# A planned attention and mixture of experts on one core: a new order for the attention, other prices for TensorE's passages, and 32 unread products of ones among the first steps

## The chip, the core and the metric

The kernel runs on one core of a Trainium2 chip. The core has five engines with a queue each: PE (TensorE, the matrix unit), DVE (VectorE), ACT (ScalarE), POOL (GpSimd) and SP (SyncE, which issues most DMAs here). An engine takes its instructions strictly in the order in which the program holds them and waits on semaphores for what the others do. The metric is the device time of one execution in microseconds (us).

## The reference

The first half is attention for 4 batches of 8 heads, 768 positions and head size 64, with a window of 128 positions and 4 positions at the start (sinks) that all see. The second half is a mixture of 8 experts over the 3072 resulting rows of 512 numbers; each row goes to its two best experts.

```python
scores = scale * np.matmul(q, k.transpose(0, 1, 3, 2))
is_sink = pos[None, :] < int(n_sink)
in_window = (rel >= 0) & (rel < int(window))
scores = np.where(is_sink | in_window, scores, -1000000000.0)
a = np.exp(scores - np.max(scores, axis=-1, keepdims=True))
a = a / (np.sum(a, axis=-1, keepdims=True) + 1e-09)
attn = np.matmul(a, v)
...
noisy_logits = x @ w_gate + np.log1p(np.exp(x @ w_noise)) * noise
top2 = np.argpartition(-noisy_logits, 2, axis=1)[:, :2]
...
h = np.maximum(x[mask] @ w1[e], 0.0)
out[mask] += top2_w[mask, k, None] * (h @ w2[e])
```

## The kernel before

**Two plans.** `phase_one` holds the attention, the routing of the first three batches, and the first loads and splits of expert 0. `phase_two` holds the routing of the last batch and the experts. Each phase lists its operations in a `Plan`: engine, duration, priority, function, what it reads and writes. `Plan.run` then plays the list through with those durations, takes on each engine the ready operation with the lowest priority number, and emits the instructions in the order of their planned starts. So the durations and the priorities (the table `PR`) set the order in which the instructions stand on every engine; on the chip that order is fixed, whatever the durations turn out to be.

**The tiles.** A group `g` is a pair of heads of one batch (16 groups); a step `n` is 256 positions of one group (48 steps, three in each group). On PE a step is:

- `turn` (T): q and k are transposed, `turn_c` on ACT copies them to `kq`, `ksink` on POOL adds the sinks' keys;
- `qk` (S): the scores, by matmuls that use 64 rows of the array, two heads at a time (kind 1 in the plan);
- `ptr` (P): the exponentials are transposed, and copied by `ptr_c` on ACT to `CT`; `ptr_m` masks them into `CM`;
- `pctr`: the sinks' part is transposed into tile X, and copied by `sink_c` on ACT to `ps`;
- `pv`: the product with v and with dv (the difference of neighbouring blocks of v, made by POOL or DVE from `vn`), by matmuls that use 64 columns of the array (kind 2), into the same tile X;
- `sinks` (kind 3): the product of `ps` with the sinks' v (`vr`), into X too; `pv_c` on ACT copies X out to `xtn`, `rows` transposes it back, `rows_c` on DVE scales it.

`vr` comes from a tile `st` that 16 small DMAs fill for each batch (`sink_values`), and two operations over all of it (`sink_hi` on ACT, `sink_lo` on DVE).

**The tile X.** `pctr`, `pv`, `sinks` and `rows` of one step write parts of one PSUM tile. The plan holds `pv` and `sink_c` for independent of each other. The program does not: the framework orders reads and writes of a tile as they are emitted. Where `pv` is emitted ahead of `sink_c`, ACT's copy waits for `pv` to end, and `sinks` waits for the copy.

**Passages.** PE's instructions have four forms: 128 rows by 128 columns (transposes, `sinks`), 64 rows (`qk`), 64 columns (`pv`), 32 columns (the gate's projection in `logits`). The plan adds a time when the kind changes, and `stay` (in `PR`) holds the engine on its kind.

**The start.** SP loads k and q of group 0 and 1, then v of group 0 and 1 (`vn`), then the 16 DMAs of `st`. One product of ones (`warm`) is issued ahead of all.

**The end of phase one.** `gather` fetches 4 tiles of rows for expert 0 after the routing of batch 2 (`place`), `rows_turn` transposes them (L947), and the first matmul of an expert is that of L1070.

Of the kernel before, what the change touches and what calls it, by code (L numbers as in the profile page):

```python
# [17 lines left out]
OP = mybir.AluOpType  # L18
AX = mybir.AxisListType
BIG = 1.0e30  # L20
PR = dict(dv_pool=2, cm_pool=10, gap=3, pc_pool=0, warm=1, cur=-28.393, cur1=3.934, cur1_0=-210.795, cur1_9=-0.214,
          cur_0=-6.435, cur_9=42.546, dv=-181.673, dv_0=-58.475, dv_9=-165.981, exps=924.339, exps_0=-284.526,
          exps_9=-135.434, ga=442.815, gt=5.527, ksink=329.474, ksink_9=351.649, lg=5.452, load_qk=4.916, load_v=-10.311,
          mins=-1.124, mins_0=-130.078, mins_9=-231.976, nosink=115.551, nosink_0=201.297, nosink_9=23.605,
          pcopy=-1100.148, pcopy_0=54.064, pcopy_9=13.8, plow=6.687, plow_0=155.036, plow_9=-170.043, prev=-313.725,
          prev_0=560.262, prev_9=8.445, ptr=-158.634, ptr_0=-7.014, ptr_9=481.977, ptr_c=113.881, ptr_c_0=180.788,
          ptr_c_9=110.108, ptr_m=-225.012, ptr_m_0=-135.409, ptr_m_9=-137.504, pv=-1.694, pv_0=1.459, pv_9=2.578,
          pv_c=-36.493, pv_c_0=-19.005, pv_c_9=0.119, qk=-419.785, qk_0=3.807, qk_9=316.006, rows=-857.853,
          rows_0=-458.314, rows_9=34.438, rows_c=-1553.261, rows_c_0=-208.37, rows_c_9=-15.709, rt=-558.501, sink_c=2.596,
          sink_c_0=-90.91, sink_c_9=-279.362, sinks=-714.907, sinks_0=-12.828, sinks_9=261.99, sub=318.235, sub_0=521.605,  # L30
          sub_9=182.999, sums=78.667, sums_0=135.936, sums_9=-1.546, sums_i=-160.405, sums_i_0=280.185, sums_i_9=-301.562,
          t0=11.199, t2=-37.957, tgroup=71.501, tgroup_0=-63.73, tgroup_9=-56.402, tgroup_c=-1595.788, tgroup_c_0=7.035,
          tgroup_c_9=-3.093, w1=579.923, ksink_0=-652.007, stay=3844.16, pctr_0=71.802, sinkv=185.095, sc_dve=2,
          pctr=-325.901, pctr_9=-655.681)
CAP = 832

CAPS = (832, 832, 832, 800, 800, 768, 768, 768)
COLD = 6.0
FIRST = 4
ZEROS = 16  # L40

# [5 lines left out]
class Plan:  # L47
# [16 lines left out]
    def get(self, tag, i, shape=None, dt=F32, pool="sb", pad=None):  # L64
        kx = (tag, i)
        if kx not in self.live:
            more = {"padded_shape": pad} if pad else {}
            self.live[kx] = self.pools[pool].tile(shape, dt, name=tag, bufs=self.rings[tag], **more)
        return self.live[kx]

    def op(self, eng, dur, prio, fn, r=(), w=(), u=(), lat=None, kind=0):


        i = len(self.ops)
        deps = set()
        for kx in list(r) + list(w) + list(u):
            if kx not in self.touch:
                self.touch[kx] = []
                self.wrote[kx] = []
            if kx[0] in self.rings:  # L80
                deps.update(self.touch.get((kx[0], kx[1] - self.rings[kx[0]]), ()))
        for kx in list(r) + list(w):
            deps.update(self.wrote[kx])
        for kx in w:
            deps.update(self.touch[kx])
        for kx in list(r) + list(w) + list(u):
            self.touch[kx].append(i)
        for kx in w:
            self.wrote[kx].append(i)
        self.ops.append((eng, dur, prio, fn, sorted(deps), lat, kind))  # L90
# [10 lines left out]
    def run(self, dry=False):  # L101
        n = len(self.ops)
        left = [len(o[4]) for o in self.ops]
        succ = [[] for _ in range(n)]
        for i, o in enumerate(self.ops):
            for d in o[4]:
                succ[d].append(i)
        at, start, free, pend = [0.0] * n, [0.0] * n, {}, {}
        kind = 0
        for i, o in enumerate(self.ops):  # L110
            free.setdefault(o[0], 0.0)
            pend.setdefault(o[0], ([], []))
            if not left[i]:
                heapq.heappush(pend[o[0]][0], (0.0, i))

        def arrive(e, t):
            wait, ready = pend[e]
            while wait and wait[0][0] <= t:
                _, i = heapq.heappop(wait)
                heapq.heappush(ready, (at[i] if e == "DMA" else self.ops[i][2], i))  # L120

        for _ in range(n):
            best = None
            for e, (wait, ready) in pend.items():
                arrive(e, free[e])
                if ready or wait:
                    t = free[e] if ready else wait[0][0]
                    if best is None or t < best[0]:
                        best = (t, e)
            t, e = best  # L130
            arrive(e, t)
            ready = pend[e][1]
            if e == "PE":
                x = min(ready, key=lambda x: (x[0] + (PR["stay"] if self.ops[x[1]][6] != kind else 0), x[1]))
                ready.remove(x)
                heapq.heapify(ready)
                i = x[1]
            else:
                _, i = heapq.heappop(ready)
            if e == "DVE" and self.ops[i][6]:  # L140
                t = max(t, free["Pool"])
            start[i] = t
            d = self.ops[i][1]
            if e == "PE":
                d = (d + (.25 if self.ops[i][6] == 1 != kind else .1 if self.ops[i][6] != kind else 0)) * (2 if t < self.cold else 1)
                kind = self.ops[i][6]
            elif e == "DVE" and self.ops[i][6]:
                free["Pool"] = t + d
            free[e] = end = t + d
            for s in succ[i]:  # L150
                lat = self.ops[i][5]
                if lat is None:
                    lat = (0 if e == "PE" else .06) if e == self.ops[s][0] else self.LAT.get((e, self.ops[s][0]), .2)
                at[s] = max(at[s], end + lat)
                left[s] -= 1
                if not left[s]:
                    heapq.heappush(pend[self.ops[s][0]][0], (at[s], s))
        self.start, self.free = start, free
        if not dry:
            for i in sorted(range(n), key=lambda i: (start[i], i)):  # L160
                if self.ops[i][3]:
                    self.ops[i][3]()
        return max(free.values())
# [20 lines left out]

def constants(nc, pool, sh):
    c = {}
    c["nz"] = pool.tile([128, sh.T, sh.E], F32, name="nz")
    jp = c["nz"].rearrange("p t e -> p (t e)")[:, :128].bitcast(I32)
    nc.gpsimd.iota(jp, pattern=[[1, 128]], base=0, channel_multiplier=-1)
    c["idf"] = pool.tile([128, 128], F32, name="idf")  # L190
    nc.vector.tensor_scalar(c["idf"], jp, 0.0, None, op0=OP.is_equal)
    c["jp"] = jp
    return c
# [6 lines left out]
def attention(tc, plan, consts, cst, sh, q, k, v, xbuf):  # L200
    nc = tc.nc
# [37 lines left out]
    def warm():  # L239

        one = cst["one"]
        nc.tensor.matmul(get("P", 0, [128, 4, 128], F32, "ps"), one, one[:, None, :].to_broadcast([128, 4, 128]),
                         start=True, stop=True)

    def sink_zero(b):
# [209 lines left out]
    for gi in range(NJ):  # L455
        for nm in nms:
            load(nm, 0, gi, -20 + gi)
    for i in range(PR.get("warm", 16)):
        op("tick", .43 if i else 1.5, i, None, r=[("t", 0)], w=[("t", 0)], lat=0)
        op("PE", .43, 1000, warm, r=[("t", 0)], w=[("P", 0)])  # L460
    for g in range(NP):
        p0 = g * NJ
        e = p0 - NJ
# [24 lines left out]
        for jj in range(NJ):  # L488
# [12 lines left out]
            if not jj:  # L501
# [13 lines left out]
               r=[("P", n + NJ) if me == "DVE" else ("CT", n)], w=[("CM", n)])  # L515
            XA[n] = xa = plan.next("X")
            op("PE", .11, n + .6 + P(g, "pctr"), lambda n=n: pctr(n), r=[("pc", n)], w=[("X", xa)])
            op("PE", .95 if jj else .7, n + .6 + P(g, "pv"), lambda n=n: pv(n),
               r=[("vn", g), ("CT", n), ("dv", g), ("CM", n), ("X", xa)], w=[("X2", xa)], kind=2)
            op("ACT", .17, n + .6 + P(g, "sink_c"), lambda n=n: sink_c(n), r=[("X", xa)], w=[("ps", n)])  # L520
            op("PE", .26, n + .6 + P(g, "sinks"), lambda n=n: sinks(n), r=[("ps", n), ("vr", g // HP)], w=[("X2", xa)], u=[("X", xa)],
               kind=3)
            op("ACT", .27, n + .6 + P(g, "pv_c"), lambda n=n: pv_c(n), r=[("X2", xa)], w=[("xt", n)], u=[("xtn", g), ("X", xa)])
            op("PE", .22, n + .7 + P(g, "rows"), lambda n=n: rows(n), r=[("xt", n), ("ps", n)], w=[("X", xa)], u=[("xtn", g)])
# [6 lines left out]
def routing_setup(nc, pool, tmp, cst, sh, w_gate, w_noise, noise):  # L531
# [19 lines left out]
    iota("dum", [128, 1], [[0, 1]], -128, 1)  # L551
    c["tri"] = tmp.tile([128, 128], BF, name="tri")
    nc.vector.tensor_scalar(c["tri"], c["jp"], 0.0, None, op0=OP.is_gt)
    c["one"] = tmp.tile([128, 128], BF, name="one")
    nc.vector.memset(c["one"], 1.0)


    c["m"] = tmp.tile([128, T + sh.FA, E], BF, name="m")
# [43 lines left out]
def logits(nc, plan, cst, sh, b, jj, z):  # L602
# [29 lines left out]
        nc.vector.tensor_reduce(get("lg", b, [128, NT, 2 * E])[:, 2 * jj:2 * jj + 2, :],  # L632
                                get(*mk).rearrange("p t h e -> p t e h"), op=OP.add, axis=AX.X)

    op("PE", .57, z, proj, r=[("xt", n) for n in ns] + [("gw", x) for x in range(4)], w=[("X", xa)], u=[("xtn", g) for g in pairs])
    op("ACT", .27, z, copy, r=[("X", xa)], w=[tk])
    op("PE", .22, z, turn, r=[tk], w=[("X", xa)])
    op("DVE", .34, z, scale, r=[("X", xa)] + [("rin", n) for n in ns], w=[mk], u=[("ri", b)])
# [750 lines left out]
```

## Time and profile before

| | |
|---|---|
| median of three runs | 801.34 us (800.09 to 804.37) |
| span of the profiled execution | 802.8 us |
| that execution's own time beside its span | not given apart; the span stands for it, 1.5 us above the median |
| PE busy in that span | 772.3 us (96%), 4753 matmuls |
| DVE, ACT, POOL busy | 434.3, 342.6, 441.5 us |
| first matmul of an expert (L1070) | 220.09 us after the start |

The views used: rows of the timeline give start, length, engine, line, operation and tiles, and in brackets how long the engine stood idle ahead of it and what ended that. Rows that follow each other are merged (x8 is eight). A matmul's shown length is its way through the array, so several overlap; what PE pays for one is the distance from start to start. An instruction on fp32 data is recorded in as many parts as the hardware makes of it, so that `pv`'s eight matmuls are sixteen records and start in pairs. Windows give for a stretch its length and the busy time of each engine in turn (PE, PE's weight loads, DVE, ACT, POOL), then PE's granted clock and the DMA's share and rate.

### The profile page before, as it was taken

To read this page: it belongs to the slowest core of one execution; us is meant where nothing else is said; L and a number is where in the kernel's file an instruction comes from. 1 tells how busy PE (TensorE), PEld (TensorE's weight loads), DVE (VectorE), ACT (ScalarE), POOL (GpSimd) and SP (SyncE) were. 2 spreads that over 40 slices of the span, in tenths; PEclk is the share of its full clock that TensorE was granted. 3 is DMA by queue.
4 is the path that set the end of the run, shared out by engine and by line. 5 is a ranking of instruction groups with operands and counts; after the bars stand their busy time and mean duration, and the time that the engine had idled before them with its cause. 6 is when DMAs were issued, how large, how long until landed. Compare 5 with 4: busy or idle time off the path is not lost.

```text
span 802.8 us, 13806 instructions
## 1 busy us (share of the span) xinstructions
PE 772.3 (96%) x4753; PEld 656.1 (82%) x4753; DVE 434.3 (54%) x1115; ACT 342.6 (43%) x695; POOL 441.5 (55%) x669
## 2 busy tenths in 40 slices
PE   7999999899798999999999999999999999999996
PEld 4776777677577888988988898899889999999994
DVE  5888897798565345354435434542553363364320
ACT  5877778686420334244233413332442343334121
POOL 5757657778604447473745456374636647366222
PEclk9999999999999999999999999999999999999998
DMA  6769767845526196264526535561744365174133
GB/s 121 169 150 200 162 155 207 181 120 129 152 90 175 22 257 152 45 140 128 102 38 158 141 56 94 144 119 37 147 123 94 73 172 121 26 175 97 32 40 40
DMA packets 151193, 96.03 MB, mean 120 GB/s; under 512 B 100528, under 2 KB 129200, under 8 KB 151120
## 3 DMA queue, kind: packets, MB, share of 16 engines
q1 hardware_dynamic: 137744, 67.93, 32.6%
q0 software_dynamic: 13376, 27.19, 19.4%
q8 instruction: 38, 0.62, 0.3%
q14 instruction: 35, 0.29, 0.1%
HBM read 66.89 MB, written 28.20 MB: 118 GB/s over the span
## 4 chain that ended last, share of the span: by engine, by line
PE 64%; issue 4%; DMA 2%; POOL 2%; DVE 1%; SPq 0%; ACT 0%; POOLq 0%; DVEq 0%; ACTq 0%
PE H L1070 11%; PE H L1072 10%; PE H L1071 10%; PE Y L1099 10%; PE Y L1101 10%; PE Y L1100 10%; POOL out L1123 1%; PE Y L1104 1%; PE Y L1105 1%; DMA xg<-x_rows,idg 1%; DMA out<-y,idx 1%; DMA st<-in_moe_w 1%; SPq L1268 0%; PE T L947 0%; PE X L616 0%
## 5 line engine op out<-in xcount | busy, mean ns | idle before, releaser
L903 POOL DMA_INDIRECT xg<-x_rows,rt_idq x174 | 175.8, 1010 | 62.1 <-issue 51.7
L1070 PE MATMUL H<-skn,w 128*128 128x384 f32 (+4 forms) x512 | 178.3, 348 | 0.0
L1072 PE MATMUL H<-skn,w 128*128 128x384 f32 (+4 forms) x512 | 176.8, 345 | 0.0
L1071 PE MATMUL H<-sqn,w 128*128 128x384 f32 (+4 forms) x512 | 176.3, 344 | 0.0
L1088 DVE SCALAR_TENSOR_TENSOR h<-H,h 128x384 fp32r<-128x384 f32 (+4 forms) x168 | 75.5, 469 | 184.7 <-ACT h L1081 184.5
L1081 ACT ACTIVATE h<-H 128x384 fp32r<-128x384 f32 (+4 forms) x128 | 64.6, 505 | 249.4 <-PE H L1072 249.3
L1132 POOL COPY spacer<-h 1x1 f32<-1x1 f32 x88 | 26.6, 303 | 167.3 <-ACT h L1081 167.1
L1123 POOL DMA_INDIRECT out<-y,idx x53 | 89.2, 1683 | 50.4 <-ACT y L1108 34.6
L1070 PEld LDWEIGHTS H<-skn,w 128*128 128x128 f32 x512 | 96.6, 189 | 7.7 <-issue 0.8
L1071 PEld LDWEIGHTS H<-sqn,w 128*128 128x128 f32 x512 | 96.6, 189 | 6.9
L1072 PEld LDWEIGHTS H<-skn,w 128*128 128x128 f32 x512 | 96.4, 188 | 3.0
L1101 PE MATMUL Y<-w2b,h 128*128 128x512 f32 x192 | 75.2, 392 | 1.1 <-DVE h L1088 1.1
L1099 PE MATMUL Y<-w2b,h 128*128 128x512 f32 x192 | 75.5, 393 | 0.6 <-ACT h L1081 0.6
L1099 PE MATMUL Y<-w2a,h 128*128 128x512 f32 x192 | 75.5, 393 | 0.0
L1100 PE MATMUL Y<-w2b,h 128*128 128x512 f32 x192 | 75.2, 392 | 0.0
L1100 PE MATMUL Y<-w2a,h 128*128 128x512 f32 x192 | 75.1, 391 | 0.0
L1101 PE MATMUL Y<-w2a,h 128*128 128x512 f32 x192 | 74.9, 390 | 0.0
L197 POOL TENSOR_TENSOR cbuf<-cbuf,mn 128x528 f32<-128x528 f32 x48 | 52.6, 1098 | 18.5 <-DVE mn L330 10.7
L310 PE MATMUL S<-kq 64*128 64x264 f32 (+1 forms) x384 | 56.4, 410 | 1.0 <-DVE ri L348 0.5
L961 ACT ACTIVATE skn<-xtn 128x512 fp32r<-128x512 f32 (+2 forms) x46 | 27.9, 606 | 63.3 <-DVE xtn L952 63.2
L197 DVE TENSOR_TENSOR w<-st,w 128x1024 fp32r<-128x1024 f32 x28 | 34.3, 1224 | 17.8 <-ACT w L1008 17.8
L1101 PEld LDWEIGHTS Y<-w2b,h 128*128 128x128 f32 x192 | 36.1, 188 | 9.4 <-DVE h L1088 1.6
(209 smaller groups left out, 1359.6 us busy)
## 6 DMA issues: line engine op xcount, KB each, us to landing
st<-in_moe_w SPq DMA_DIRECT2D x36, 512.0 KB
st<-in_moe_w SPq DMA_DIRECT2D x112, 128.0 KB
out<-zt SPq DMA_DIRECT2D x31, 256.0 KB
vn<-in_v SPq DMA_DIRECT2D x16, 384.0 KB
x_rows<-xr SPq DMA_DIRECT2D x48, 128.0 KB
kn<-in_k SPq DMA_DIRECT2D x30, 192.0 KB
qn<-in_q SPq DMA_DIRECT2D x30, 192.0 KB
xg<-x_rows,rt_idq POOLq DMA_INDIRECT x174, 2.9
```

The source lines that it names most:

```text
L197: eng.tensor_tensor(out, a, b, op=OP.subtract)
L310: nc.tensor.matmul(p[:, :2 if j else 1], kq(g)[r, j // 2, 2 + j % 2, NS:], x[:, :2 if j else 1], start=True, stop=True)
L903: nc.gpsimd.indirect_dma_start(out=x[:, i, :], out_offset=None, in_=xbuf.rearrange("r (q d) -> (r q) d", d=sh.SW), in_offset=bass.Indirect ...
L1070: nc.tensor.matmul(p, w[:, 0, i], xh, start=(i == 0), stop=False)
L1071: nc.tensor.matmul(p, w[:, 0, i], xl, start=False, stop=False)
L1072: nc.tensor.matmul(p, w[:, 1, i], xh, start=False, stop=(i == DC - 1))
L1081: nc.scalar.activation(get("h", FC * q + f, [128, 2 * 128 * FIRST], F32R)[:, :width], get("H", FC * q + f), AF.Relu)
L1088: nc.vector.scalar_tensor_tensor(h[:, o:o + s1 - s0], p[:, s0:s1], 0.0, h[:, s0:s1].bitcast(F32), op0=OP.max, op1=OP.subtract)
L1099: nc.tensor.matmul(p, hh, w[:, 0], start=(f == 0), stop=False)
L1100: nc.tensor.matmul(p, hh, w[:, 1], start=False, stop=False)
L1101: nc.tensor.matmul(p, hl, w[:, 0], start=False, stop=(f == FC - 1))
L1123: d = nc.gpsimd.indirect_dma_start(out=out, out_offset=bass.IndirectOffsetOnAxis(ap=c["idx"][:size(e, t), e, t:t + 1], axis=0), in_=get("y ...
```

## The change

`PR` gets other numbers throughout; for steps 0, 1 of every eight `pcopy` is on POOL and not on ACT (`pc_pool=2`: 12 of 48). The plan's price of a passage becomes .2 us into `qk` and .15 us otherwise, kind 0 and 3 count as one, and the gate's projection counts as kind 2. `ones` is written first of all on DVE, and 32 products of ones, which nobody reads, are put into PE's list with the worst priority; each may be planned .215 us after the one ahead of it, and so they fill places in which the plan sees PE idle. They write a tile of the ring X that is used by no step.

```diff
-PR = dict(dv_pool=2, cm_pool=10, gap=3, pc_pool=0, warm=1, cur=-28.393, cur1=3.934, cur1_0=-210.795, cur1_9=-0.214,
+PR = dict(dv_pool=2, cm_pool=10, gap=3, pc_pool=2, cur=-316.098, cur1=74.576, cur1_0=389.469, cur1_9=0.0, cur_0=0.0,
...
-COLD = 6.0
+COLD = 5.0
+WARM = 32
...
-                x = min(ready, key=lambda x: (x[0] + (PR["stay"] if self.ops[x[1]][6] != kind else 0), x[1]))
+                x = min(ready, key=lambda x: (x[0] + (PR["stay"] if self.ops[x[1]][6] % 3 != kind % 3 else 0), x[1]))
...
-                d = (d + (.25 if self.ops[i][6] == 1 != kind else .1 if self.ops[i][6] != kind else 0)) * (2 if t < self.cold else 1)
+                d = (d + (0 if self.ops[i][6] % 3 == kind % 3 else .2 if self.ops[i][6] == 1 else .15)) * (2 if t < self.cold else 1)
...
+    c["one"] = pool.tile([128, 128], BF, name="one")
+    nc.vector.memset(c["one"], 1.0)
...
-        nc.tensor.matmul(get("P", 0, [128, 4, 128], F32, "ps"), one, one[:, None, :].to_broadcast([128, 4, 128]),
+        nc.tensor.matmul(get("X", first, [128, 4, 128], F32, "ps"), one, one[:, None, :].to_broadcast([128, 4, 128]),
...
-    for i in range(PR.get("warm", 16)):
-        op("tick", .43 if i else 1.5, i, None, r=[("t", 0)], w=[("t", 0)], lat=0)
-        op("PE", .43, 1000, warm, r=[("t", 0)], w=[("P", 0)])
+    first = plan.next("X")
+    for i in range(WARM):
+        op("tick", .215 if i else 1.2, i, None, r=[("t", i - 1)], w=[("t", i)], lat=0)
+        op("PE", .215, 1e6, warm, r=[("t", i)], u=[("X", first)])
...
-            op("PE", .95 if jj else .7, n + .6 + P(g, "pv"), lambda n=n: pv(n),
+            op("PE", .87 if jj else .65, n + .6 + P(g, "pv"), lambda n=n: pv(n),
...
-    op("PE", .57, z, proj, r=[("xt", n) for n in ns] + [("gw", x) for x in range(4)], w=[("X", xa)], u=[("xtn", g) for g in pairs])
+    op("PE", .45, z, proj, r=[("xt", n) for n in ns] + [("gw", x) for x in range(4)], w=[("X", xa)], u=[("xtn", g) for g in pairs],
+       kind=0 if last else 2)
```

The lines of the changed kernel are two further down from `attention` on (L310 becomes L312). From the last projection of the gate in phase one on, PE's order is the same row for row in both kernels.

**The start, on SP.** The loads of v (`vn`) and of `st` trade places. Before:

```order
L267 DMA kn<-in_k 128x6x64 x2
L267 DMA qn<-in_q 128x6x64 x2
L271 DMA vn<-in_v 128x12x64 x2
L250 DMA st<-in_v 4x4x64 x16
L267 DMA kn<-in_k 128x6x64 x2
```

And after:

```order
L269 DMA kn<-in_k 128x6x64 x2
L269 DMA qn<-in_q 128x6x64 x2
L252 DMA st<-in_v 4x4x64 x16
L273 DMA vn<-in_v 128x12x64
L269 DMA kn<-in_k 128x6x64 x2
```

The sixteen small loads now stand ahead of v of group 0, and v of group 1 stands behind k and q of group 2.

**The first steps, on PE** (P is `ptr`, X<-pcbuf is `pctr`, X<-CT and X<-CM are `pv`, X<-ps is `sinks`). Before:

```order
L368 MATMUL P<-idf,cbuf 128x128 x4
L394 MATMUL X<-CT,vn 64x128 x4
L397 MATMUL X<-CM,dv 64x128 x2
L310 MATMUL S<-kq 128x264 x4
L385 MATMUL X<-idf,pcbuf 128x128
L394 MATMUL X<-CT,vn 64x128 x4
L397 MATMUL X<-CM,dv 64x128 x4
L406 MATMUL X<-ps,vr 128x128 x4
```

And after, from the last of the 32 products of ones on (five of them stand between the third P and this `pctr`):

```order
L244 MATMUL X<-one 128x512
L387 MATMUL X<-idf,pcbuf 128x128
L396 MATMUL X<-CT,vn 64x128 x4
L399 MATMUL X<-CM,dv 64x128 x2
L396 MATMUL X<-CT,vn 64x128 x4
L399 MATMUL X<-CM,dv 64x128 x4
L408 MATMUL X<-ps,vr 128x128 x4
```

The two steps' `pv` stand together, and the scores of step 4 no longer stand ahead of them.

**The last steps, on PE** (T<-xg is `rows_turn`, X<-xtn is `rows`). Before:

```order
L385 MATMUL X<-idf,pcbuf 128x128
L394 MATMUL X<-CT,vn 64x128 x4
L397 MATMUL X<-CM,dv 64x128 x4
L406 MATMUL X<-ps,vr 128x128 x2
L368 MATMUL P<-idf,cbuf 128x128 x4
L419 MATMUL X<-idf,xtn 128x128 x2
L385 MATMUL X<-idf,pcbuf 128x128
L394 MATMUL X<-CT,vn 64x128 x4
L397 MATMUL X<-CM,dv 64x128 x2
L406 MATMUL X<-ps,vr 128x128 x2
L419 MATMUL X<-idf,xtn 128x128 x2
```

And after:

```order
L387 MATMUL X<-idf,pcbuf 128x128
L396 MATMUL X<-CT,vn 64x128 x4
L399 MATMUL X<-CM,dv 64x128 x4
L387 MATMUL X<-idf,pcbuf 128x128
L408 MATMUL X<-ps,vr 128x128 x2
L396 MATMUL X<-CT,vn 64x128 x4
L399 MATMUL X<-CM,dv 64x128 x2
L408 MATMUL X<-ps,vr 128x128 x2
L421 MATMUL X<-idf,xtn 128x128 x4
L370 MATMUL P<-idf,cbuf 128x128 x4
```

Where each step ran through by itself, two steps now lie in each other: another step's `pctr` stands between a `pv` and its `sinks`, and `rows` come two steps at a time.

More of the change, by code (lines that the diff above doesn't have):

```diff
@@ L20 @@
 BIG = 1.0e30
-PR = dict(dv_pool=2, cm_pool=10, gap=3, pc_pool=0, warm=1, cur=-28.393, cur1=3.934, cur1_0=-210.795, cur1_9=-0.214,
[L22 to L34, printed above, removed]
@@ new lines @@
+PR = dict(dv_pool=2, cm_pool=10, gap=3, pc_pool=2, cur=-316.098, cur1=74.576, cur1_0=389.469, cur1_9=0.0, cur_0=0.0,
+          cur_9=-338.706, dv=3.697, dv_0=-3440.041, dv_9=-5.252, exps=1433.695, exps_0=14.943, exps_9=-47.365,
+          ga=261.653, gt=590.016, ksink=102.577, ksink_9=-11.086, lg=0.317, load_qk=0.0, load_v=-0.697, mins=36.093,
+          mins_0=683.429, mins_9=58.706, nosink=6.145, nosink_0=366.642, nosink_9=-4.22, pcopy=-25.182,
+          pcopy_0=877.155, pcopy_9=-7.293, plow=8.138, plow_0=-19.886, plow_9=-223.574, prev=0.0, prev_0=-19.364,
+          prev_9=0.0, ptr=0.655, ptr_0=-69.919, ptr_9=-0.248, ptr_c=-19.131, ptr_c_0=9.758, ptr_c_9=0.0, ptr_m=-794.5,
+          ptr_m_0=-408.279, ptr_m_9=186.738, pv=606.544, pv_0=-415.362, pv_9=170.355, pv_c=-3.043, pv_c_0=0.0,
+          pv_c_9=5.912, qk=-228.31, qk_0=-195.444, qk_9=299.15, rows=0.0, rows_0=437.256, rows_9=408.894,
+          rows_c=-2103.315, rows_c_0=517.963, rows_c_9=0.0, rt=-680.773, sink_c=-36.416, sink_c_0=35.85,
+          sink_c_9=12.309, sinks=-332.739, sinks_0=-432.619, sinks_9=393.682, sub=65.273, sub_0=-820.977,
+          sub_9=74.172, sums=120.291, sums_0=-696.415, sums_9=977.753, sums_i=0.0, sums_i_0=584.662, sums_i_9=-20.343,
+          t0=-29.656, t2=12.759, tgroup=1036.947, tgroup_0=2.026, tgroup_9=0.0, tgroup_c=323.737, tgroup_c_0=11.405,
+          tgroup_c_9=561.666, w1=1204.601, ksink_0=-1177.388, stay=3039.256, pctr_0=0.0, pctr=-574.631, pctr_9=-0.362)
@@ L517, in attention @@
             op("PE", .11, n + .6 + P(g, "pctr"), lambda n=n: pctr(n), r=[("pc", n)], w=[("X", xa)])
-            op("PE", .95 if jj else .7, n + .6 + P(g, "pv"), lambda n=n: pv(n),
+            op("PE", .87 if jj else .65, n + .6 + P(g, "pv"), lambda n=n: pv(n),
                r=[("vn", g), ("CT", n), ("dv", g), ("CM", n), ("X", xa)], w=[("X2", xa)], kind=2)
             op("ACT", .17, n + .6 + P(g, "sink_c"), lambda n=n: sink_c(n), r=[("X", xa)], w=[("ps", n)])
-            op("PE", .26, n + .6 + P(g, "sinks"), lambda n=n: sinks(n), r=[("ps", n), ("vr", g // HP)], w=[("X2", xa)], u=[("X", xa)],
+            op("PE", .22, n + .6 + P(g, "sinks"), lambda n=n: sinks(n), r=[("ps", n), ("vr", g // HP)], w=[("X2", xa)], u=[("X", xa)],
                kind=3)
@@ L553, in routing_setup @@
     nc.vector.tensor_scalar(c["tri"], c["jp"], 0.0, None, op0=OP.is_gt)
-    c["one"] = tmp.tile([128, 128], BF, name="one")
-    nc.vector.memset(c["one"], 1.0)
     c["m"] = tmp.tile([128, T + sh.FA, E], BF, name="m")
```

## The prediction

> **What bounds the kernel now.** I read the page's busy times and chain first, then windows by stage, then PE's rows where a stage loses time.
>
> ```profile
> span 802.8 us, 13806 instructions
> PE 772.3 (96%) x4753; PEld 656.1 (82%) x4753; DVE 434.3 (54%) x1115; ACT 342.6 (43%) x695; POOL 441.5 (55%) x669
> PE 64%; issue 4%; DMA 2%; POOL 2%; DVE 1%; SPq 0%; ACT 0%; POOLq 0%; DVEq 0%; ACTq 0%
> ```
> ```profile
> 0.00:22.70 22.70, 17.26 (x91) 10.27 (x91) 14.14 (x38) 12.32 (x26) 13.58 (x37) 1.00 0.66 131
> 22.70:198.00 175.30, 168.90 (x1665) 127.34 (x1666) 151.20 (x414) 133.53 (x353) 122.59 (x237) 1.00 0.70 163
> 198.00:220.00 22.00, 15.53 (x150) 11.83 (x148) 13.42 (x34) 9.68 (x23) 13.77 (x18) 0.92 0.54 153
> 220.00:802.80 582.80, 570.63 (x2855) 506.67 (x2851) 255.58 (x631) 187.09 (x294) 291.52 (x380) 0.99 0.47 105
> ```
>
> PE carries everything. The experts (last row) keep the order they have, so what the attention saves moves them forward whole, and what it loses moves them back; their one long wait, for rows gathered after the last routing, hangs on their own start. The attention has three stages: a head with 5.4 us of idle PE, a middle with 6.4 us in 175, and a tail with 6.5 us in 22. In the middle DVE is busy for 151.2 of 175.3 us (86%): there is little room above PE.
>
> **Passages.** The distance from start to start says what PE pays.
>
> ```profile
> 24.79 1.16 PE L310 MATMUL S<-kq 64*128 64x264 f32 x8
> 25.88 0.66 PE L419 MATMUL X<-idf,xtn 128*128 128x128 f32 x4
> 26.37 0.60 PE L368 MATMUL P<-idf,cbuf 128*128 128x128 f32 x4
> 26.81 0.38 PE L283 MATMUL T<-idf,kn 128*128 128x128 f32 x2
> 27.02 0.38 PE L283 MATMUL T<-idf,qn 128*128 128x128 f32 x2
> 27.24 0.27 PE L385 MATMUL X<-idf,pcbuf 128*128 128x128 f32 x1
> 27.45 0.66 PE L394 MATMUL X<-CT,vn 128*64 128x128 f32 x8
> 27.93 0.61 PE L397 MATMUL X<-CM,dv 128*64 128x128 f32 x8
> 28.47 0.33 PE L385 MATMUL X<-idf,pcbuf 128*128 128x128 f32 x1
> 28.64 0.38 PE L283 MATMUL T<-idf,kn 128*128 128x128 f32 x2
> ```
>
> Four transpositions P take .44 us (26.37 to 26.81), .11 each, and T follows for nothing. Into `pv` there is .10 more (27.24 to 27.45 for one of .11) and about .04 within its first eight (.48 for four pairs of .11): .15. Back, .10 (27.93 to 28.47) and .06 (28.47 to 28.64): .16. Scores: four pairs of 264 columns should take .90 by the same rate and take 1.09, which is some .10 at each end, and with the .10 ahead of the entry a passage into them is .2. In PE's rows up to the first L1070 I count 190 passages before, 50 of them into scores, and 176 after, 54 into scores. That is 50 x .2 + 140 x .15 = 31.0 us against 54 x .2 + 122 x .15 = 29.1: **1.9 us off PE**. Passages between 64 and 32 columns, six after and one before, may cost nothing: up to .8 more.
>
> **Copies behind `pv`.** Where `sink_c` is emitted after its step's `pv`, ACT waits for `pv` and `sinks` for ACT:
>
> ```profile
> 120.28 0.61 PE L397 MATMUL X<-CM,dv 128*64 128x128 f32 x8
> 120.94 0.28 ACT L401 ACTIVATE ps<-X 128x128 fp32r<-128x128 f32 x1 [0.65 <-PE X L397]
> 121.27 0.44 PE L406 MATMUL X<-ps,vr 128*128 128x128 f32 x2 [0.38 <-ACT ps L401]
> ```
> ```profile
> ACT ps L401 <- PE X L397: 17.7, 20, 2.5
> ```
>
> `pv`'s four pairs need .44 and the way out .10; `sinks` starts .99 after them, so .45 are lost, and .06 in its first record: .5. In the order of the built programs `sink_c` stands behind its `pv` in 22 of 48 steps before, and in 8 of these `sinks` follows `pv` with nothing between: five in the middle, three in the tail. After, it is 8 steps, and two with nothing between, one in each stage. So the middle gets 4 x .5 = 2.0 back. The second row says that ACT stood 17.7 us behind `pv` in all; all that is queued behind the copy (exponentials, CT, the copies of S) came late too, and with 8 such steps for 22 most of that goes. Of the 4 us of idle PE in the middle that these five do not explain I take 1.4 us as gained. **Middle: 3.4 us**, between 0 (other waits take their place, DVE first) and 6.4 (all idle time).
>
> **The tail.**
>
> ```profile
> 203.89 0.28 ACT L401 ACTIVATE ps<-X 128x128 fp32r<-128x128 f32 x1 [2.47 <-PE X L397]
> 206.15 0.69 DVE L378 TENSOR_TENSOR CM<-P,ge 128x512 f32<-128x512 f32 x1 [3.46 <-ACT CT L371]
> 211.75 0.28 ACT L401 ACTIVATE ps<-X 128x128 fp32r<-128x128 f32 x1 [2.31 <-PE X L397]
> 215.29 0.63 PE L947 MATMUL T<-idf,xg 128*128 128x128 f32 x4 [0.67 <-PE X L385]
> 217.33 0.66 PE L947 MATMUL T<-idf,xg 128*128 128x128 f32 x4
> 219.53 0.64 PE L616 MATMUL X<-xtn,wbd 128*32 128x256 f32 x8 [1.26 <-DVE sqn L197]
> ```
> ```profile
> 210.50:213.90 3.40, 3.03 (x23) 2.63 (x20) 2.58 (x8) 1.52 (x5) 0.78 (x2) 0.51 0.81 211
> ```
>
> Here the late copies do most harm: ACT stands 2.5 and 2.3 us, DVE behind it 3.5, PE is idle for 6.5 and then runs 3.4 us at half its clock (0.51), which costs 1.7: 8.2 in all. After, two steps lie in each other. What stays or is new: the wait ahead of the last projection, 1.3; the third and fourth L947, which stand .2 us of PE work apart where the tile's way over ACT and DVE took 2.04 from start to start (215.29 to 217.33), so some 1.4; two pairs of P with only a `pctr` between, whose copy on ACT takes .6, some 1.5 for both; one late copy, .5. That makes 4.7, **a gain of 3.5 us**. It is 0 if a new chain through the gathers decides (POOL's four follow the same routing product), and 6.9 if only the last wait stays.
>
> **The head.** Two things change.
>
> ```profile
> 7.28 2.69 PE L310 MATMUL S<-kq 64*128 64x132 f32 x12
> 9.89 0.69 PE L283 MATMUL T<-idf,kn 128*128 128x128 f32 x2
> 10.37 0.64 PE L283 MATMUL T<-idf,qn 128*128 128x128 f32 x2
> 10.94 3.51 PE L310 MATMUL S<-kq 64*128 64x264 f32 x12
> 14.38 1.11 PE L368 MATMUL P<-idf,cbuf 128*128 128x128 f32 x4
> 17.62 0.66 PE L368 MATMUL P<-idf,cbuf 128*128 128x128 f32 x4
> 23.97 0.89 PE L406 MATMUL X<-ps,vr 128*128 128x128 f32 x4
> ```
>
> Two T's take .48 here (9.89 to 10.37) and .21 later (26.81 to 27.02), and four P's show 1.11 at 14.38 and .66 at 17.62: up to some 16 us PE runs at half its clock, though the windows' clock column says 1.00. The products of ones keep PE at work from about 1.2 us (ones is now DVE's first work; SP starts at .93 in the row below). They are 128x512, .21 us at the full clock and .43 at half. When the clock comes free then, no row says. It came free after 3.4 us in the tail and in the head some 8.7 us after the scores at 7.28 began, from which on no long wait stands in the rows; so between 4.6 and 10.
>
> By PE's rows, up to the end of the `sinks` of steps 0 and 1 there are 18.1 us at the full clock, 6.9 of them ones. Up to the time t at which the clock comes free, (t - 1.2) / 2 of them is done, and the rest follows at the full clock, so they end at t + 18.1 - (t - 1.2) / 2 = 18.7 + t/2: 21.0 to 23.7. Before, they ended at 24.8 (the row of 23.97), but with one step's scores (1.2 us) done besides; the mark is 24.8 - 1.2 = 23.6. So PE alone would gain up to 2.6.
>
> The other thing is `st`.
>
> ```profile
> 0.93 0.98 SPq L267 DMA_DIRECT2D kn<-in_k  x2
> 9.35 2.40 SPq L271 DMA_DIRECT2D vn<-in_v  x2
> 11.86 7.29 SPq L250 DMA_DIRECT2D st<-in_v  x16
> 21.30 1.05 ACT L254 ACTIVATE vr<-st 128x1024 fp32r<-128x1024 f32 x1
> ```
>
> Its 16 DMAs now start at 9.35 and end between 14.8 (at .34 each, most of them) and 16.6; they land 2.1 later at most (19.15 to 21.30). ACT's queue has `vr` ahead of the exponentials of step 2, which stood behind it before: 16.9 to 18.7, then 1.05 + .6 (a copy of T) + .64, and P of step 2 comes at 19.2 to 21.0. Behind it stand five products of ones (1.1), `pctr`, two `pv`, `sinks`: 4 us, an end at 23.2 to 25.0. v of group 0 goes out behind `st` as well, lands by some 19, and dv needs 1.55 on POOL: no later than that. So the wait for `st` takes what the clock would give: **the head loses .5**, between a gain of 2.6 and, if the clock stays at half all through (37.4), a loss of 13.8.
>
> **Edits with no price of their own.** 12 copies go from ACT to POOL, which is at 70% in the middle. The later priority of expert 0's weights moves splits on ACT and POOL that end ahead of the first expert in both orders. Were POOL's not done, L1070 would wait for them.
>
> **The sum.** 1.9 + 3.4 + 3.5 - .5 = 8.3 us off the profiled execution: 802.8 - 8.3 = 794.5. That execution lies 1.5 above the median of the runs (801.3), so 793.0.
>
> **The rivals.**
>
> - *Only the passages count.* The waits in middle and tail are those of a pipeline whose DVE is 86% busy; taken from ACT they come back as waits for DVE (in the list of PE's waits DVE hardly stands now, which speaks against it). Then 1.9 - .5 = 1.4: 799.9. Chance .14.
> - *Products of ones at half clock ahead of real work* (the other side). Each stands in PE's queue and costs .43 there. With the clock held until t the sinks end at 18.7 + t/2 against 23.6, and the other gains, 8.8, are eaten at t = 27.4. Held all through, 13.8 - 8.8 = 5.0 lost: 806.3. Against it: in the tail 3.4 us sufficed. Chance .05.
> - [...] Chance .12.
> - *Middle and tail lose nearly no time any more*: 5.5 and 6 gained: 788.1. Chance .14.
>
> [...]
>
> **How the numbers follow.** The forecast, with sizes of its terms between half and one and a half, has .50 and a range of 789 to 797; other mixtures of small losses make the last .05, at 802 to 808. A measurement of this kernel tells about .5% (4 us) from no change. Below 797.3 are the forecast, the third rival for the most part, the fourth: .76. Within 4 us are the first and edges of the others: .17. Above 805.3: .07. The range that leaves out 2 in 10 goes from 786 to 801.
>
> **What would show it.** Right: L1070 first at about 212; T's of .21 from about 7 us on; ACT's waits for `pv` ahead of L403 near 6 us; tail windows at a full clock; DVE at about 89% in the middle. Wrong: a first `pv` later than 22 us with ones right ahead of it, new waits of PE for DVE in the middle of several us, or L949's first row held by the gathers.

## The result, and the profile after

The changed kernel takes 797.07 us (median of 16 runs, 794.56 to 801.82), the kernel before 804.46 (16 runs, 800.09 to 808.76): ratio 0.9918, with a 95% interval of 0.9900 to 0.9936. By the ratio that is 6.6 us off (the two medians lie 7.4 apart), where 8.3 were forecast. The time of 797 lies in the range given (786 to 801), though 4 above the 793 named: the three runs of before that were shown have a median 3.1 below that of all 16.

The profiled executions differ by more, 802.8 against 795.4. The page of the changed kernel:

```profile
span 795.4 us, 13881 instructions
PE 772.5 (97%) x4784; PEld 654.8 (82%) x4784; DVE 436.0 (55%) x1115; ACT 341.3 (43%) x683; POOL 439.0 (55%) x681
PE 80%; issue 5%; DVE 4%; POOL 3%; DMA 3%; ACT 3%; SPq 1%; POOLq 0%; DVEq 0%; ACTq 0%
```

PE is as busy as before (772.5 for 772.3) though 6.9 us of products of ones have come in. Windows by stage, cut at four events that both have: the start of the last of the first four `sinks` (steps 0 and 1), the routing product of batch 2 (the matmul `rt_tc,rt_op`), the first expert's matmul, the end. First before, then after (columns as in the prediction: length, then PE, weight loads, DVE, ACT and POOL; near the end PE's granted clock):

```profile
0.00:24.60 24.60, 19.15 (x111) 11.73 (x111) 15.94 (x41) 12.96 (x28) 15.48 (x39) 1.00 0.71 138
24.60:201.76 177.16, 169.27 (x1670) 127.75 (x1671) 152.12 (x415) 134.31 (x355) 123.52 (x238) 1.00 0.69 162
201.76:220.09 18.33, 13.35 (x126) 9.96 (x123) 10.70 (x30) 8.26 (x19) 11.03 (x15) 0.91 0.55 157
220.09:802.80 582.71, 570.54 (x2855) 506.67 (x2851) 255.58 (x631) 187.09 (x294) 291.43 (x380) 0.99 0.47 105
```
```profile
0.00:23.90 23.90, 20.82 (x133) 11.70 (x134) 14.03 (x38) 11.89 (x23) 13.19 (x40) 1.00 0.65 135
23.90:195.62 171.72, 167.82 (x1679) 126.99 (x1679) 154.88 (x417) 133.85 (x347) 125.05 (x250) 1.00 0.72 169
195.62:214.07 18.45, 13.89 (x126) 9.72 (x123) 11.71 (x31) 8.46 (x20) 11.39 (x15) 0.88 0.58 172
214.07:795.40 581.33, 569.95 (x2855) 506.39 (x2851) 255.37 (x630) 187.09 (x294) 289.39 (x378) 1.00 0.45 104
```

The head ends .7 earlier, but without the scores (1.2 us) that before had done by then: .5 lost. The middle is 5.4 shorter, with those scores in it: 6.6 gained. From the routing product to the first expert's matmul nothing moved: 18.33 against 18.45. The experts are 1.4 shorter. The sum is .5 - 6.6 + .1 - 1.4 = -7.4. In the middle PE's idle time falls from 7.9 to 3.9 us (length less busy time); the other 2.6 are less busy time, once the scores' 1.2 are counted on both sides.

The middle: ACT's list of waits up to 220 us, whose first row before was 17.7 us for `pv` ahead of the copy of the sinks' part:

```profile
ACT xtn L416 <- PE X L408: 10.3, 16, 1.4
ACT ps L403 <- PE X L399: 8.6, 7, 1.9
```

It has fallen to half (8.6; near 6 was expected), and `sinks` waits for that copy .8 us in all (two times) for 3.0 (eight times) before.

The head: PE's rows, and POOL's for `dv`:

```profile
1.25 3.17 PE L244 MATMUL X<-one 128*128 128x512 bf16 x7 [1.25 <-DVE one L188]
4.21 0.63 PE L285 MATMUL T<-idf,kn 128*128 128x128 f32 x2
5.10 1.24 PE L244 MATMUL X<-one 128*128 128x512 bf16 x5
...
19.73 1.24 PE L244 MATMUL X<-one 128*128 128x512 bf16 x5
21.03 0.33 PE L387 MATMUL X<-idf,pcbuf 128*128 128x128 f32 x1
21.29 0.66 PE L396 MATMUL X<-CT,vn 128*64 128x128 f32 x8
22.28 0.44 PE L399 MATMUL X<-CM,dv 128*64 128x128 f32 x4 [0.34 <-POOL dv L199]
```
```profile
20.69 1.54 POOL L199 TENSOR_TENSOR dv<-vn 128x640 f32<-128x640 f32 x1 [3.91 <-DMA vn<-in_v]
```

Seven products take 3.17 us (.43 each), the five at 5.10 take 1.24 (.21 each): the clock came free at about 4.9 us, where before it took until 16 (two T's .42 apart at 15.29, .27 at 16.92). Yet the end of the head moved little: POOL stood idle for 3.9 us until v of group 0 had landed, and `pv` waited for `dv`.

The tail: PE's rows from the routing product on.

```profile
195.62 0.47 PE L814 MATMUL X<-rt_tc,rt_op 128*128 128x56 f16 x12
...
202.25 0.75 PE L949 MATMUL T<-idf,xg 128*128 128x128 f32 x4 [0.89 <-DMA xg<-x_rows,idg]
...
206.83 0.66 PE L949 MATMUL T<-idf,xg 128*128 128x128 f32 x4 [0.33 <-DVE sqn L199]
...
208.96 0.60 PE L949 MATMUL T<-idf,xg 128*128 128x128 f32 x4
...
211.02 0.63 PE L949 MATMUL T<-idf,xg 128*128 128x128 f32 x4 [1.23 <-issue]
213.06 1.08 PE L617 MATMUL X<-xtn,wbd 128*32 128x256 f32 x8 [1.42 <-DVE sqn L199]
```

The four L949 stand 6.6, 11.2, 13.3 and 15.4 us behind the routing product. Before it was 6.4, 10.8, 13.5 and 15.6 (L947 at 208.21, 212.57, 215.29, 217.33; routing product at 201.76). The chain over this stage begins with the gather, 5.21 us from its issue until its rows are there, just ahead of the first L949:

```profile
197.00 5.21 DMA xg<-x_rows,idg
```

From the first L949 to the second it is 4.6 us, and about 2.1 from each to the next behind that. ACT copies the first gathered tile out of T (`skn`) only behind a late copy of the sinks' part, which waits for its `pv`, and that `pv` runs at half clock (.51 from 202.60 to 206.10):

```profile
205.17 0.28 ACT L403 ACTIVATE ps<-X 128x128 fp32r<-128x128 f32 x1 [1.56 <-PE X L399]
205.46 0.59 ACT L963 ACTIVATE skn<-T 128x512 fp32r<-128x512 f32 x1
```

### The profile page after: what moved, and what is told of

Read it like the earlier page. It is cut to its first block, busy times and chain, and to the rows that moved or that the text cites. A ratio compares the mean times of both kernels' runs of the same rounds, so it can differ in the third digit from the quotient of the medians.

```text
span 795.4 us, 13881 instructions
## 1 busy us (share of the span) xinstructions
PE 772.5 (97%) x4784; PEld 654.8 (82%) x4784; DVE 436.0 (55%) x1115; ACT 341.3 (43%) x683; POOL 439.0 (55%) x681
## 4 chain that ended last, share of the span: by engine, by line
PE 80%; issue 5%; DVE 4%; POOL 3%; DMA 3%; ACT 3%; SPq 1%; POOLq 0%; DVEq 0%; ACTq 0%
PE H L1072 11%; PE H L1074 10%; PE H L1073 10%; PE Y L1101 10%; PE Y L1103 10%; PE Y L1102 10%; PE S L312 4%; PE X L396 3%; PE X L399 2%; PE P L370 2%; PE T L285 2%; DMA xg<-x_rows,idg 1%; POOL out L1125 1%; PE X L408 1%; PE Y L1106 1%
## 5 line engine op out<-in xcount | busy, mean ns | idle before, releaser
L1134 POOL COPY spacer<-h 1x1 f32<-1x1 f32 x88 | 26.3, 299 | 172.2 <-ACT h L1083 172.0
L199 POOL TENSOR_TENSOR cbuf<-cbuf,mn 128x528 f32<-128x528 f32 x48 | 51.0, 1066 | 18.1 <-DVE mn L332 15.9
L312 PE MATMUL S<-kq 64*128 64x264 f32 (+1 forms) x384 | 54.1, 395 | 0.0
```

The lines of the kernel that those rows point to most:

```text
L199: eng.tensor_tensor(out, a, b, op=OP.subtract)
L312: nc.tensor.matmul(p[:, :2 if j else 1], kq(g)[r, j // 2, 2 + j % 2, NS:], x[:, :2 if j else 1], start=True, stop=True)
```

## The experiments

Each run's median, its ratio to the kernel before in the same set with its 95% interval, two events of its profiled execution, and the mean granted clock of its timed runs:

| run | us | ratio | routing product | first expert's matmul | mean clock |
|---|---|---|---|---|---|
| changed kernel | 797.07 | .9918 (.9900 to .9936) | 195.62 | 214.07 | .9942 |
| a_noones | 794.50 | .9886 (.9862 to .9910) | 195.02 | 212.54 | .9972 |
| a_first7 | 795.57 | .9891 (.9859 to .9922) | 195.87 | 213.44 | .9947 |
| a_tailones | 794.39 | .9888 (.9866 to .9911) | 196.05 | 213.69 | .9970 |
| a_tailturns | 795.23 | .9903 (.9876 to .9929) | 196.07 | 213.74 | .9965 |
| a_ring | 796.34 | .9920 (.9888 to .9951) | 196.07 | 212.07 | .9937 |
| a_copies | 800.30 | .9966 (.9945 to .9987) | 196.19 | 216.31 | .9926 |
| b_copies | 804.85 | 1.0014 (.9999 to 1.0028) | 204.35 | 223.24 | .9914 |
| a_free | 797.44 | .9914 (.9883 to .9945) | 194.60 | 214.64 | .9916 |
| b_free | 799.27 | .9938 (.9913 to .9963) | 197.68 | 215.91 | .9932 |
| a_same | 798.23 | .9957 (.9933 to .9982) | 198.50 | 217.73 | .9945 |
| a_cross | 812.40 | 1.0109 (1.0079 to 1.0138) | 211.04 | 229.69 | .9965 |
| best | 793.00 | .9860 (.9830 to .9891) | 195.22 | 211.46 | .9955 |

Names with a_ start from the changed kernel, with b_ from the one before. A thousandth of clock goes with some .7 us (the slope over the 16 runs of the changed kernel). The sets were taken apart from each other, so ratios compare better between them than medians do; the whole interval lies clear of the changed kernel's in best, a_copies, b_copies and a_cross alone. Up to the routing product four of these programs are alike (changed kernel, a_tailones, a_tailturns, a_ring) and have it between 195.62 and 196.07: a difference of .5 there is no finding.

**a_noones: what the products of ones bring.**

```diff
-        op("PE", .215, 1e6, warm, r=[("t", i)], u=[("X", first)])
+        op("PE", .215, 1e6, None, r=[("t", i)], u=[("X", first)])
```

> The changed kernel without its 32 products of ones (they leave the output untouched); every other instruction in its place. Theory (the ones free the clock at 4.65 us): without them T's stand .48 apart up to 12 us or later, the sinks of steps 0 and 1 end at 26 instead of 24.2, and the time is 2 us more than the changed kernel's 797. Rival (the head waits for v of group 0, which lands at 20.7 whatever PE does): dv still ends at 22.2, the sinks end within .5 of 24.2, the time stays within 1 us. Third possibility: the five ones that stand behind the last P at 19.7 cost more than the clock brings, and the time falls by 1 us.

```profile
7.39 2.68 PE L312 MATMUL S<-kq 64*128 64x132 f32 x12
10.01 0.69 PE L285 MATMUL T<-idf,kn 128*128 128x128 f32 x2
10.49 0.63 PE L285 MATMUL T<-idf,qn 128*128 128x128 f32 x2
...
14.43 0.38 PE L285 MATMUL T<-idf,kn 128*128 128x128 f32 x2
...
20.13 0.27 PE L387 MATMUL X<-idf,pcbuf 128*128 128x128 f32 x1
...
21.68 0.44 PE L399 MATMUL X<-CM,dv 128*64 128x128 f32 x4 [0.69 <-POOL dv L199]
```

The clock is late again (T's .48 apart at 10.01), and nothing is lost by it: `pctr` stands at 20.13 instead of 21.03, and PE waits for `dv` in both. `sinks` starts at 22.92 (23.52 with ones) and ends at 23.4 (24.0). The theory that the freed clock shortens the head has fallen. Of the rival, one half holds: v of group 0 sets the end of the head. The other half, that v lands at 20.7 whatever PE does, doesn't:

```profile
19.49 2.13 POOL L199 TENSOR_TENSOR dv<-vn 128x640 f32<-128x640 f32 x1 [0.94 <-DMA vn<-in_v]
```

Here `dv` starts at 19.49 and ends at 21.6 instead of 22.2, and this is the .6 by which `sinks` is earlier; the five ones ahead of `pctr` (the third possibility) do not set it, since PE waits for `dv` behind them. In the eight profiles with all 32 products `dv` starts between 20.4 and 21.1, in a_first7 at 19.6, though SP issues the load at 15.6 to 15.8 in this run, in a_first7 and in the changed kernel alike. So the later 25 products go with a later v; in what way is not shown. The median is 2.6 lower, more than the .6 of the head; 2.1 of it would go with the higher clock (.9972 for .9942), and the intervals of the two ratios overlap.

**a_first7: the early ones alone.** Only the first 7 of the 32 are emitted (`warm if i < 7 else None`).

> The changed kernel with the first 7 of its 32 products of ones (PE at work from 1.25 us) and without the other 25. Head: the sinks of steps 0 and 1 hang on v of group 0, so they end as without any ones (23.3 to 23.9), whatever the clock was. Clock: if the places of the half-clock stretches are counted from PE's first work, the mean clock of the runs falls back to about .994 and the time is 796 to 797; if not, it stays at .997 and 794.5, as without ones.

`sinks` ends at 22.9, earlier than with all (24.0) and than with none (23.4), a little outside the range expected; PE waits .63 for `dv` as without. The mean clock is .9947, as in the changed kernel; the median is 1.5 lower (795.57), with intervals that overlap, and its profile has no half-clock stretch in the tail. That the stretches' places are counted from PE's first work is not borne out: PE begins at 1.2 us in the changed kernel, a_copies, a_free and a_same, and their first stretches begin at 202.7, 203.6, 201.9 and 205.9, not at whole stretches of 3.41 us from each other.

**a_tailones and a_tailturns: the clock in the tail.** Unread work in PE's idle places ahead of the first and the fourth L949 and behind the fourth; m is 5 each time for products of ones, 10 for transpositions.

```diff
+    def fill(m):
+        o = get("S", 96, [128, 2, 512], F32, "ps")
+        for j in range(m):
+            nc.tensor.matmul(o[:, 0, :]..., cst["one"], cst["one"]..., start=True, stop=True)
# a_tailturns:
+            nc.tensor.transpose(o[:, 0, :128], cst["idf"], cst["idf"])
```

> The changed kernel with 15 more products of ones at the end of the attention: five ahead of the first L949 (where PE is idle for .89), five ahead of the fourth (1.23), five behind it (1.42). Theory (a stretch in which PE has only transpositions and waits lowers its clock): the two half-clock stretches at 202.8 and 213.0, 3.4 us and 1.7 us of loss each, disappear and the time falls by 2.5 to 3.4 us, to some 794. Rival (the tail's end is set by the gathers and the one T tile): the clock is full there, but the first expert's matmul comes less than 1 us earlier; 796.5.

> As the run with ones in the tail, with 30 unread transpositions of fp32 in the places of the 15 products: as long (.11 each for .21), PE as busy. If transpositions count for PE's clock like other work, both half-clock stretches disappear as with ones, and the time is the same as with ones. If they don't, the stretches stay as in the changed kernel, and the time is within 1 us of its 797.

Windows of the changed kernel show the half clock, and behind it the tail of a_tailones as a whole:

```profile
202.60:206.10 3.50, 3.50 (x26) 2.66 (x24) 0.90 (x3) 1.89 (x5) 0.64 (x3) 0.51 0.59 182
212.90:216.40 3.50, 3.34 (x14) 2.08 (x15) 0.44 (x2) 0.38 (x1) 0.00 (x0) 0.51 0.82 259
```
```profile
196.05:213.69 17.64, 15.15 (x141) 10.04 (x138) 11.61 (x31) 8.38 (x20) 11.37 (x15) 1.00 0.58 174
```

At full clock the tail takes 17.64 for 18.45: of some 2.2 us of half-rate loss ahead of the first expert's matmul (1.7 of the first stretch, .5 of the second) .8 came back there; the rest of the first was slack behind the chain. Another 1.0 of the second stretch fell on the experts. The median falls by 2.7, inside the 2.5 to 3.4 of the theory; but a_noones has no fill in its tail and runs at full clock there too (17.52). With the fills it was so each time: six runs between 793.75 and 794.83 at clocks of .996 to .998, where the 16 of the changed kernel spread from .989 to .998, and the six of a_ring, with the same start and no fill, from .990 to .998. That the fills are what does it isn't shown by this alone: the six runs of a_noones, without any, are at .996 to .998 as well. Transpositions do nearly as much (.994 to .998); with six runs each, whether they count less than products is not settled.

**a_ring: the one tile T.**

```diff
-        o, x = get(ring, ti, [128, c, 128], F32, "ps"), get("xg", n)
+        o, x = get("S", 96 + t, [128, 2, 512], F32, "ps")[:, 0, :]..., get("xg", n)
```

> The changed kernel with the four L949 tiles in the two free tiles of the scores instead of the one tile T; order untouched. Theory (the tail is a chain: routing product, gather, four passes through the one tile T of 2.05 us each): PE's waits ahead of the fourth L949 (1.23) and part of that ahead of the last projection (1.42) go, the first expert's matmul comes 1.3 to 2.5 us earlier, 795. Rival (the copies on ACT and DVE, which the four still share, set the pace): less than .5 us earlier, 797.

```profile
208.52 0.60 PE L954 MATMUL S<-idf,xg 128*128 128x128 f32 x4
...
209.46 0.63 PE L954 MATMUL S<-idf,xg 128*128 128x128 f32 x4
211.50 0.64 PE L617 MATMUL X<-xtn,wbd 128*32 128x256 f32 x8 [1.41 <-DVE sqn L199]
```

The third and fourth (L954 here) stand .94 apart and no longer 2.06. The stage takes 16.0 us against 17.6 at the same clock: 1.6 shorter, as the theory has it. So the one tile T is part of the tail's chain: two more tiles shorten it by 1.6 us. The median hardly shows it (796.34): the clock was at .990 to .992 in three of six runs, and the experts' wait for the gathered rows was 1.9 there for .6 in a_tailones.

**b_copies and a_copies: the copy's place.** `pairs` holds `sink_c` and `pv` of each step. Where the copy of the sinks' part was planned behind its `pv`, its planned start is set to just ahead of it.

```diff
+        for i, j in self.pairs:
+            if start[i] > start[j]:
...
+                start[i] = start[j] - 1e-6
```

> The kernel before, with one thing moved: where ACT's copy of the sinks' part stands behind its step's pv (22 of 48 steps) it is written directly ahead of that pv. Durations, priorities and every other row stay. Theory (the late copies are what the middle and the tail lose): ACT's waits for pv ahead of that copy fall from 17.7 us to under 3, the 8 gaps of .5 ahead of sinks go, and the first expert's matmul comes 3.5 to 6 us earlier; 797 to 799 where the kernel before has 802 to 804. Rival (a pipeline whose DVE is at 86% gives the time back): the gaps ahead of sinks go, others grow, less than 1.5 us.

> The changed kernel with its 8 late copies of the sinks' part written ahead of their pv; the rest stays. Theory: the 8.6 us that ACT stands behind pv go; one of them holds up the copy of the first gathered tile at the end of the attention (1.56), so that the chain through the tile T starts earlier: 1 to 2.5 us off the changed kernel's 797. Rival (the chain from the routing product over the gathers to T sets the end, and the copies are beside it): less than .5 us.

```profile
PE X L399 <- ACT ps L406: 9.0, 21, 0.8
```

The row is from PE's waits in b_copies up to 222 us; L399 is the first half of `pv` there, L406 the copy. The wait has changed sides: written ahead, the copy holds up `pv`, 21 times, since both are in tile X. The routing product comes 2.6 later than before. A half-clock stretch of 6.8 us (23.7 to 30.5) has cost up to 3.4 of that; without it the edit would have gained .8 at most, where 3.5 were expected. a_copies is no better: 4.4 us of such waits, and a half-clock stretch of 6.8 us in the tail. The theory as I had put it (the late place costs, the early one is free) has fallen. The rival had the outcome (the gaps ahead of `sinks` go, others grow), though the time came back as waits for ACT and not for DVE. My reading is that what counts is whether there is other work for PE between `pctr` and `pv`, long enough for the copy; no run tests it by itself.

**b_free and a_free: the coupling itself.**

```diff
-        nc.scalar.activation(get("ps", n, ...), get("X", XA[n])[:, 2, :], AF.Copy)
+        nc.scalar.activation(get("ps", n, ...), pcbuf[:, n % plan.rings["pc"], :]..., AF.Copy)
```

> The kernel before, with the copy of the sinks' part taken from the sinks' part ahead of its transposition (pcbuf) and not from tile X: the copy and pv no longer stand in one tile, and neither waits for the other. It leaves the sinks' share out of the result as the reference has it. Theory (the copy and pv in one tile are what the order before loses time to): the routing product of batch 2 comes 3 to 5 us earlier than at 201.8, most of the 6.1 us by which the changed kernel has it earlier. Rival (the gain in the middle has other sources: DVE's waits, the places of the routing): less than 1 us earlier.

> The same edit in the changed kernel (the sinks' share is left out likewise). Theory: it has little of this wait left, so the routing product comes .5 to 1.5 us earlier than at 195.6, and the difference between the two kernels shrinks from 6.1 to 2.5 to 4 us, of which passages are 2.2. Rival: both kernels gain alike, and the difference stays at 6.

The routing product comes at 197.68 for 201.76 and at 194.60 for 195.62: 4.1 and 1.0 us earlier, both as the theory has them, and b_free has a half-clock stretch at 24 to 27 us on top, which may have cost it up to 1.7. Half of the 6.1 us between the two kernels (3.1, or up to 4.8 without that stretch) goes with this coupling, and 3.1 (or down to 1.4) are left; passages were reckoned at 1.9. The copy itself is no shorter from `pcbuf` (.30 to .31 us for .28), but it no longer waits for `pctr` either; such waits are 1.6 us in the changed kernel up to the routing product, and none is in the profile of the one before. In time, too, the kernel before gains by it (.9938) and the changed one doesn't (.9914 for .9918).

**a_same and a_cross: the price of a passage.** One unread transposition more per step, behind `pctr` or between the halves of `pv`.

```diff
# a_same, in pctr; a_cross, in pv ahead of its second half
+        nc.tensor.transpose(x[:, 3, :], idf, idf)
```

> The changed kernel with 48 unread transpositions more, one behind each pctr, where the form of the matmul stays the same. At .11 each that is 5.2 us of PE; idle time takes up 1 to 2 of it: 800 to 802.

> The same 48 unread transpositions, but each between the two halves of a pv, so that the form changes twice more in each step: 96 passages more than in the run with the form kept. Theory (a passage costs .15): 14.4 us more than that run, 814 to 816. Rival (passages are free where PE's next weights are loaded ahead, and the gaps beside them in the rows are waits): within 4 us of it. If the price is .10 as the table before had it, 9.6 us more.

In a_cross the attention's values are not the reference's: the transposition writes another part of the tile between the halves of `pv`, and why that changes the sums is not shown. The run serves for its times alone. The difference between the two is 14.2 us by the medians and 12.5 by the routing product, for 96 passages: .15 and .13 each. The rows show it too, .26 between the transposition and the next half, .11 of which is its own:

```profile
101.86 0.66 PE L398 MATMUL X<-CT,vn 128*64 128x128 f32 x8
102.45 0.33 PE L393 MATMUL X<-idf 128*128 128x128 f32 x1
102.71 0.66 PE L401 MATMUL X<-CM,dv 128*64 128x128 f32 x8
```

The same 48 transpositions where the form stays cost 2.9 us by the routing product and 1.2 by the medians, less than their 5.2, since idle places take them up. The waits do not grow: between 24 us and the routing product PE's busy time goes from 172.0 to 184.8 us, and its idle time from 2.5 to 2.2. Passages are a price of PE's own, and no wait for another engine.

**best: what the runs point to.** No ones at the start, v of group 0 loaded ahead of `st`, the score tiles for the gathered rows, 11 products of ones in the tail.

> The changed kernel without the 32 products of ones, v of group 0 loaded ahead of the 16 DMAs of st, the four L949 tiles in the free tiles of the scores, and 11 products of ones at the end of the attention (five ahead of the first L949, six behind the fourth). From the run without ones (794.5): .7 less in the head (PE's wait for dv goes), 1.5 less in the tail as in the run with the score tiles: 792.3. If the rows gathered for the last tiles of expert 0 land no earlier, half of that is given back there: 793.4.

It has the lowest median, 793.0 (.9860), and its interval ends below the one of the changed kernel; the intervals of a_noones, a_tailones, a_first7 and others overlap with it. The tail takes 16.24. The head gained nothing (`sinks` at 22.99): PE's wait for `dv` is gone, but `st`, now behind v, lands later, and the copy of T that stands behind `vr` on ACT comes late instead:

```profile
18.49 1.06 ACT L258 ACTIVATE vr<-st 128x1024 fp32r<-128x1024 f32 x1 [0.68 <-DMA st<-in_v]
```
```profile
20.09 0.44 PE L287 MATMUL T<-idf,kn 128*128 128x128 f32 x2 [0.98 <-ACT kq L293]
```

## Why the prediction held, and where it failed

- **Passages, 1.9 us:** right. The price of .15 that was read from start to start is .13 to .15 in a_cross, and 14 passages fewer (four more of them into scores) give about that. PE's busy time in the middle fell by 2.6, which leaves room for the "up to .8 more" of that step; no run separates it.
- **Copies behind `pv` and the middle, 3.4 us:** right in size and cause, incomplete in mechanism. Up to the routing product 6.6 us were gained, against 1.9 + 3.4 and the part of the tail's waits that lay ahead of that product (198 to 201.8). PE's idle time there fell by 4.0. The coupling of copy and `pv` is worth 3.1 of the gain or more, as b_free and a_free show. That a copy behind `pv` costs .5 and one ahead of it nothing is wrong; b_copies turned it into waits of `pv`.
- **The tail, 3.5 us:** this step failed; behind the routing product .1 is lost. I added up the waits that would go, each at its length. The step named its own lower bound: nothing, if a chain through the gathers decides. That was the case: routing product, 5.2 us of gather, four passes through T. L949's first row waited .89 for the gather, which the prediction had named as a sign of being wrong. The one late copy that was left, put at .5, stood 1.56 us in the chain, ahead of the copy out of T. The half clock that was to go came back as well, at 202.6 and 212.9.
- **The head, .5 lost:** the size was right, and the reason only in part. `st` on ACT was late as described (1.1 us of wait ahead of `vr`), but the last wait was the one for v: it landed at 20.7, where I had written by some 19; without the later products of ones it was there at 19.5 and 19.6.
- **The clock at the start:** free at 4.9 us, near the lower end of 4.6 to 10. So the third rival (free at 16 us as before, 795.6) and that of a clock held all through fell. No run shows why it should take until 16 us with the ones ahead; the rows show 4.9 us with them and, in a_noones, T's still .48 apart at 10.01 without them. The free clock was worth nothing, since PE does not set the head's end.
- **What was not forecast, 1.4 us in the experts:** the wait for the rows gathered after the last routing is shorter, and no half-clock stretch follows it (before, 258.3 to 261.7). First before, then after:

```profile
257.46 0.66 PE L947 MATMUL TX<-idf,xg 128*128 128x128 f32 x4 [2.75 <-DMA xg<-x_rows,idg]
```
```profile
251.43 0.66 PE L949 MATMUL TX<-idf,xg 128*128 128x128 f32 x4 [1.76 <-DMA xg<-x_rows,idg]
```

The runs without a profile agree: those of the kernel before have a mean clock of .9919 to .9930 in the three sets, those of the changed kernel .9942, which goes with .8 to 1.6 us by the slope above. This hid part of the missing tail. So the sum came near by luck in part: of the tail's 3.5 us nothing came, and 1.3 more in the middle than the 1.9 + 3.4, with the 1.4 of the experts, made up for most of it. The rival "only the passages count" (1.4 us) fell with the middle, and "hardly any time lost" (13 us) with the tail; its own terms (1.9 + 5.5 + 6 - .5 = 12.9) make 788.4 and not 788.1.

## What to carry to other kernels

A wait that is seen in a stage is worth its length only if the chain behind it doesn't wait for something else: cut the stage at an event that both kernels have (here the routing product), and read the chain from there on. In these runs a copy and a product that share a tile waited for each other whichever was written first (the copy 17.7 us for `pv` in the kernel before, `pv` 9.0 us for the copy in b_copies); another source for the copy took the wait away in b_free, and other work between the two may do as well (not tested). Fillers for the clock belong, if anywhere, where the runs show it at half, and not where PE waits for a transfer anyway; a run without any fillers, as a_noones, tells whether they are needed.

## What the runs showed of the hardware

While PE has work, the half clock that the clock column shows came in stretches of 3.4 us (202.68 to 206.10 in the changed kernel) or twice that (23.7 to 30.5 in b_copies). In one execution they lie on a grid: in the kernel before they begin at 210.5 and 258.3 (47.8 us apart, 14 times 3.41), in the changed one at 202.7 and 212.9 (3 times), in b_copies at 23.7 and 221.6 (58 times), in b_free at 24.0, 201.5 and 300.4 (52 and 29 times). What sets its start is not shown.

PE was not idle all through the time ahead of them. The last 3.4 us ahead of the two stretches of the changed kernel:

```profile
199.27:202.68 3.41, 2.20 (x16) 1.49 (x15) 2.46 (x9) 2.29 (x5) 3.07 (x5) 1.00 0.98 298
209.50:212.92 3.42, 0.92 (x7) 0.47 (x5) 1.78 (x5) 1.19 (x2) 0.94 (x2) 1.00 0.49 122
```

PE was busy for 2.20 of 3.41 in the first, with no pause over .9 us, 12 of its 16 records transpositions, and the clock fell to .51. Ahead of the second it was busy for .92 of 3.42. Which of the pauses and the transpositions lowers the clock is not shown: a_noones has the same order there, and its clock stays at 1.00 (17.52 us from the routing product to the first expert's matmul).

The spread between runs of one program goes with the clock: in the 16 runs of the changed kernel the time goes from 794.6 at a mean clock of .998 to 801.8 at .989. One stretch of 3.4 us at half clock lowers the mean over 797 us by .002 and costs up to 1.7 us, .8 for each thousandth; the slope of .7 fits that. Where the stretches lie in the runs without a profile isn't shown.
